# Retention and Fourier-mix kernel on one core: the first batch's constants, DFT tables, scores, folds and mean are rearranged

## The chip, the core and the metric

One core of one Trainium2 chip runs the whole kernel in one launch. Its five engines have queues of their own and are synchronised by semaphores: TensorE (PE, matrix multiply; PEld is its weight load), VectorE (DVE), ScalarE (ACT), GpSimd (POOL) and SyncE (SP), which issues most of the transfers. Sixteen DMA engines move data between HBM and the on-chip memory SBUF; matrix products land in PSUM, in banks[...]. The metric is the device time of one execution in microseconds, as a median over executions. A profile is one more execution, recorded by the hardware.

## The reference

Inputs are q, k, v of shape (4 batches, 8 heads, 768 steps, 64) and two weights, 512 x 2048 and 2048 x 512. The first half is a retention recurrence with one decay per head; the second is a Fourier token mix and a two-layer MLP:

```python
gamma = 1.0 - 2.0 ** (-5.0 - np.arange(H))
for t in range(S):
    state = gamma * state + einsum('bhd,bhe->bhde', k[:, :, t], v[:, :, t])
    y[:, :, t] = (1 / sqrt(D)) * einsum('bhd,bhde->bhe', q[:, :, t], state)
x = y.transpose(0, 2, 1, 3).reshape(B, S, H * D)         # (4, 768, 512)
u = x + np.real(fft(fft(x, axis=1), axis=2))
un = (u - mean(u)) / sqrt(var(u) + 1e-6)                 # over the 512 channels
out = u + np.maximum(un @ w_ch1, 0) @ w_ch2
```

## The kernel before

All four batches run one after another, each in two parts that overlap with the neighbours' parts.

**Attention.** Heads are taken in pairs, so that 2 x 64 channels fill 128 partitions, in the order 0, 3, 1, 2 (`PAIR_ORDER`, L30). The sequence is cut into 6 chunks of 128 steps. For each pair `load_unit` (L91) loads q, k and v, 384 KB each, on SyncE's queue. `cast_unit` (L233) turns them into 16-bit q16, kd (k times a decay per step, from `gexp`) and v16; this runs on GpSimd, but for q of batches 1 to 3, which ScalarE casts (L250) into `q16z`, a layout in which each head has a 128-wide block with zeros in the other head's half. `t_unit` (L261) transposes q and kd: in batch 0 on TensorE through PSUM with a ScalarE copy back, in batches 1 to 3 by DMA on SyncE's queue (L267, L269). `a_unit` (L284) forms the scores of two chunks: because qTz holds zeros in the other head's rows, one 128-row matmul with 256 columns gives both heads, and VectorE multiplies by `maskp`, the causal mask times a decay per head, into `atm`. `kv_unit` (L300) forms the chunk states s16 by a chain of VectorE updates. `y_unit` (L326) adds the part from earlier chunks (qT times s16) and the part within the chunk (atm times v16), and ScalarE scales the sum into x (L349). The 512 channels of x lie on two "sides": 0 holds channels 0 to 256 upward, 1 holds 512 to 256 downward, so that channel c and 512 - c stand at the same place.

**Fourier part.** `fold_unit` (L355) uses the symmetries of a real transform: sums and differences of the two halves of the sequence (`xab`, L367), then of the two sides (`eo`, L371), in two column blocks (columns 0 to 129, and 130 to 257). Stage 1, `s1_unit` (L376), multiplies eo by cosine and sine tables over the sequence (`csp`, `ssp`) into g, and VectorE reverses g into g16r. `g0_unit` (L394) does channel 0 with another layout of the cosines, `csn`. Stage 2, `s2_unit` (L418), multiplies g by the channel tables (`cd16`, `sd16`) for one block of 128 rows, forms u in two VectorE operations, adds x on VectorE or GpSimd (L448, L450), takes mean and variance (`bn_stats`, `bn_aggr`, L453, L454) and lets ScalarE write `un` = mean - u (L456). In batch 0 the first three blocks are transposed on TensorE (`unT_unit`, L472), all others by DMA on SyncE's queue.

**MLP.** `h0_unit` (L505; the first three blocks of batch 0) and `h_unit` (L490) form the first layer in PSUM, relu alternates between ScalarE and VectorE. `ch_unit` (L525) accumulates the second layer over 16 matmuls of 512 columns, scales by 1/sigma from `rstd_unit` (L463) and stores.

**What sets the order.** The program is written as units. At the start come the loads of batch 0 and the constants, then all `trig` units (the five DFT table units: three VectorE operations, an absolute value and two sines on ScalarE each, in four temporary buffers used in turn; and a GpSimd copy that makes csn from csp), then `attn_units(0)`, pair after pair, the weight loads, and the first three stage-2 blocks. From then on `emit` (L596) merges the units of the MLP of batch b, of the attention of batch b + 1 and of their stage 2 by a fraction of the MLP's course. The tile framework takes this order as a priority and makes the order of each engine's queue from it with a plan of its own in which every instruction starts once its inputs are ready; so a unit can stand ahead of one that was written before it. `issue_after` (L242, L544, L553) ties an instruction to a place behind another on its engine: the first casts of batch 1 behind the third block of stage 2, the weight loads (on GpSimd's queue) behind the last casts of batch 0. The loads of batch 1 wait for weight loads, by a dependency that is set by hand (L98 to L102).

The lines that build the zero fills and the constants on the engines before (GpSimd memsets and iotas, ScalarE's maskp) are L113 to L166 and L211 to L227.

## Time and profile before

| | us |
|---|---|
| median of 3 executions | 285.1 (284.24 to 285.47) |
| the profiled execution's time | 284.21 |
| its span, first to last instruction | 282.4 |
| TensorE busy | 235.9 (84%) |
| VectorE busy | 179.1 (63%) |
| ScalarE busy | 111.7 (40%) |
| GpSimd busy | 74.0 (26%) |

The page cuts the span into 40 slices of 7.06 us; a digit is the busy share of a slice in tenths. The lines in order of time read: start in us, duration in us, engine, line of the kernel, operation, what is written <- what is read, shapes, number of instructions merged into the line, and in brackets how long the engine had been idle and what ended that. Ends of TensorE's matmuls are modelled. SPq is SyncE's queue of transfers: a line there is the time in which the transfer was issued, not that in which the data moved.

### The profile page before, as it was taken

The page shows a single profiled execution, that of the slowest core. Times are in us where ns is not written, and L with a number is a line of the kernel's source. Part 1 is how long each engine was busy: PE and PEld are TensorE (multiplying, and loading weights), DVE is VectorE, ACT ScalarE, POOL GpSimd, SP SyncE. Part 2 cuts the span into 40 slices and gives each one's busy share as a digit, 9 for nine tenths or more (in the row PEclk, how much of TensorE's full clock was granted, in tenths as well). Part 3 has the DMA queues.
Part 4 walks back from the last instruction along what each step waited for, and adds up shares of the span by engine and source line. Part 5 has one row for each costly group of instructions (what it writes and reads, how often), then busy time and mean ns, then how long its engine had stood idle before and what let it go on. Part 6 is the DMA issues. An engine that isn't in the chain of part 4 may idle for free.

```text
span 282.4 us, 4877 instructions
## 1 busy us (share of the span) xinstructions
PE 235.9 (84%) x1840; PEld 147.6 (52%) x1840; DVE 179.1 (63%) x424; ACT 111.7 (40%) x228; POOL 74.0 (26%) x145
## 2 busy tenths in 40 slices
PE   1138565749998899979997999989999999899994
PEld 0027453739665565456555654556566546445541
DVE  7666586356296886878768884498788735623421
ACT  4956734264433443545421661244224513511300
POOL 5678300166031122534213041131000501300000
PEclk9999957595999999999999999999999999999999
DMA  9999999999759999599999982134610031112001
GB/s 169 218 218 160 204 192 214 220 218 185 150 121 226 230 222 166 116 231 175 214 244 205 193 161 75 75 67 102 95 74 2 19 111 39 37 56 78 0 37 75
DMA packets 122039, 39.50 MB, mean 140 GB/s; under 512 B 114848, under 2 KB 118944, under 8 KB 122016
## 3 DMA queue, kind: packets, MB, share of 16 engines
q1 hardware_dynamic: 117792, 35.01, 63.5%
q0 software_dynamic: 4224, 4.19, 9.3%
q8 instruction: 14, 0.23, 0.4%
q14 instruction: 9, 0.07, 0.1%
HBM read 27.26 MB, written 6.29 MB: 119 GB/s over the span
## 4 chain that ended last, share of the span: by engine, by line
PE 54%; DVE 17%; ACT 12%; DMA 6%; issue 5%; POOL 3%; SPq 1%; POOLq 0%; ACTq 0%; DVEq 0%
PE psc L532 24%; PE psh L495 14%; PE psh L512 3%; PE wkA L292 3%; DMA qTz<-q16z 3%; PE ps L383 3%; DVE bst L453 2%; DMA q<-in_q_dram 2%; POOL u L450 2%; DVE eo L371 2%; DVE xab L367 2%; DVE atm L294 2%; ACT x L349 2%; PE wkY L337 2%; DVE ht L501 1%
## 5 line engine op out<-in xcount | busy, mean ns | idle before, releaser
L532 PE MATMUL psc<-w,ht 128*128 128x512 f16 x384 | 88.8, 379 | 0.7 <-DVE ht L501 0.7
L495 PE MATMUL psh<-unT,w 128*128 128x384 f16 x448 | 82.7, 326 | 2.3 <-DMA unT<-un 1.5
L532 PEld LDWEIGHTS <-ht 128*128 128x128 f16 x384 | 36.1, 98 | 38.9 <-issue 1.9
L495 PEld LDWEIGHTS <-w 128*128 128x128 f16 x448 | 41.9, 98 | 27.6 <-issue 5.3
L499 ACT ACTIVATE ht<-psh 128x384 f16<-128x384 f32 x56 | 27.3, 489 | 56.9 <-PE psh L495 56.7
L294 DVE TENSOR_TENSOR atm<-wkA,maskp 128x512 f16<-128x512 f32 x48 | 32.7, 684 | 13.3 <-PE wkA L292 13.2
L501 DVE TENSOR_SCALAR ht<-psh 128x384 f16<-128x384 f32 x56 | 30.6, 548 | 9.9 <-PE psh L495 9.9
L536 DVE SCALAR_TENSOR_TENSOR ob<-psc,stats,u 128x512 f32<-128x512 f32 x24 | 17.9, 744 | 29.4 <-PE psc L532 29.4
L448 POOL TENSOR_TENSOR u<-u,x 128x256 f32<-128x256 f32 x21 | 13.4, 637 | 86.6 <-DVE u L442 84.2
L292 PE MATMUL wkA<-qTz,kT 128*128 128x256 f16 x96 | 19.7, 298 | 12.5 <-ACT kT L281 10.9
L252 POOL TENSOR_SCALAR kd<-k,gexp 128x384 f16<-128x384 f32 x32 | 18.7, 595 | 32.9 <-PE wkK L310 8.0
L456 ACT ACTIVATE un<-u,stats 128x512 f16<-128x512 f32 x24 | 17.2, 720 | 22.8 <-DVE stats L454 18.9
L349 ACT ACTIVATE x<-wkY,gexp 128x384 f16<-128x384 f32 x32 | 16.9, 582 | 20.1 <-PE wkY L341 20.0
L450 POOL TENSOR_TENSOR u<-u,x 128x256 f32<-128x256 f32 x24 | 15.6, 650 | 30.4 <-DVE u L444 26.8
L453 DVE BATCH_NORM_STATS2 bst<-u 128x6 f32<-128x512 f32 x24 | 16.6, 694 | 9.4 <-POOL u L450 9.2
L320 DVE SCALAR_TENSOR_TENSOR s<-s,gk,wkK 128x128 f16<-128x128 f16 x64 | 21.7, 339 | 0.5
L337 PE MATMUL wkY<-s,qTz 128*128 128x64 f16 x160 | 17.5, 199 | 4.1 <-DVE s L320 2.9
L337 PEld LDWEIGHTS <-qTz 128*128 128x128 f16 x160 | 13.8, 103 | 11.8 <-issue 4.4
L292 PEld LDWEIGHTS <-kT 128*128 128x128 f16 x96 | 9.5, 105 | 18.5 <-ACT kT L281 11.5
L255 POOL TENSOR_SCALAR v<-v 128x768 f16<-128x768 f32 x16 | 13.6, 847 | 19.4 <-DMA v<-in_v_dram 19.4
L442 DVE SCALAR_TENSOR_TENSOR u<-pq,g,qn 128x257 f32<-128x257 f32 x24 | 11.5, 477 | 10.6 <-ACT qn L439 10.6
L512 PE MATMUL psh<-unT,w 128*128 128x128 f16 x192 | 15.3, 258 | 3.4 <-ACT unT L484 2.5
(101 smaller groups left out, 253.4 us busy)
## 6 DMA issues: line engine op xcount, KB each, us to landing
q<-in_q_dram SPq DMA_DIRECT2D x16, 384.0 KB, 6.1
k<-in_k_dram SPq DMA_DIRECT2D x16, 384.0 KB, 6.2
v<-in_v_dram SPq DMA_DIRECT2D x16, 384.0 KB, 6.2
out_dram<-ob SPq DMA_DIRECT2D x24, 256.0 KB, 2.2
w<-in_moe_w_ch_dram POOLq DMA_DIRECT2D x8, 512.0 KB, 10.9
unT<-un SPq DMA_TRANSPOSE x21, 2.4
qTz<-q16z SPq DMA_TRANSPOSE x12, 4.1
kT<-kd SPq DMA_TRANSPOSE x12, 2.9
```

Source lines behind the costliest of these rows:

```text
L292: nc.tensor.matmul(wk[:, c2], st["kT"][:, c, :], st["qT"][:, c], start=True, stop=True)
L294: nc.vector.tensor_tensor(out=st["atm"][:, 2 * part:2 * part + 2], in0=wk, in1=maskp[:, PAIR_ORDER[i]].unsqueeze(1).to_broadcast([P, 2, 2, ...
L320: nc.vector.scalar_tensor_tensor(out=s16[:, c], in0=s16[:, c - 1], scalar=gk128[:, hp:hp + 1], in1=wk[:, c - c0], op0=ALU.mult, op1=ALU.add)
L337: nc.tensor.matmul(yk[h2][:, c, :], qT[:, c, h2, :], s16[:, c - 1, sl], start=(c == 1), stop=False, skip_group_check=True)
L349: nc.scalar.activation(dst, yk[h2], AF.Copy, bias=0.0, scale=gq8[:, h:h + 1])
L450: xadd = nc.gpsimd.tensor_tensor(out=u[:, kb, 256:512], in0=u[:, kb, 256:512], in1=x[:, kb, 1, 257:1:-1], op=ALU.add)
L453: nc.vector.bn_stats(bst, u[:, kb, :])
L495: nc.tensor.matmul(psh, w116[:, cb, fb * P:(fb + 1) * P], unT[:, cb, rt * 384:(rt + 1) * 384], start=(cb == 0), stop=(cb == 3))
L499: nc.scalar.activation(ht16[:, fb, :], psh, AF.Relu, bias=0.0, scale=-1.0)
L501: nc.vector.tensor_scalar(out=ht16[:, fb, :], in0=psh, scalar1=-1.0, scalar2=0.0, op0=ALU.mult, op1=ALU.max)
L512: nc.tensor.matmul(psh[:, f], w116[:, cb, fb * P:(fb + 1) * P], unT[:, cb, kb * P:(kb + 1) * P], start=(cb == 0), stop=(cb == 3))
L532: nc.tensor.matmul(psc, ht16[:, fb, rb3 * P:(rb3 + 1) * P], w216[:, fb, :], start=(fb == 0), stop=(fb == NFB - 1))
```

## The change

The edits concern batch 0 and the constants.

- **Constants over the engines.** Fewer index patterns on GpSimd (one instruction for several columns); the memsets of `lgrow`, `gk128` and `maskf` go to VectorE; the decay table `gexp` comes ahead of the identity, of the long index row `kf` and of the other constants. The eight ScalarE copies that make `maskp` and the zero fills of `q16z` move into `late_consts`, written after the third stage-2 block; the zero fills of `qTz` are dropped (the DMA transposes of q16z write the zeros). Six small VectorE operations for row parity move into `parity_consts`, behind pair 1.
- **DFT tables between the pairs.** Ten temporary buffers in place of four; two table units after each of the pairs 0 and 1, one after pair 2. csn is made by three more sines on ScalarE in place of the GpSimd copy.
- **Row-tiled scores.** In batch 0 q is transposed without zeros by one ScalarE copy for both heads; each head's scores are a 64-row matmul of 128 columns (head 0 in partitions 0 to 63, head 1 in 64 to 127) into a PSUM bank of its own, three chunks at a time, and VectorE multiplies by a constant and the plain mask `maskf`. The state part of y is done on 64 rows too.
- **Folds by side.** The fold is split into `fold_s` (sums and differences of the sequence halves, for given columns and sides) and `fold_d`. In batch 0 everything that does not need the last pair is folded before the last pair's y. Batches 1 to 3 do the same operations as before.
- **Mean from sums of x.** For the first three blocks the mean of u is computed as (sum of x) / 512 plus the channel-0 spectrum g0. ScalarE sums x while copying it to a scratch tile; `bn_stats` and `bn_aggr` for the three blocks move into `rstd_unit`, ahead of the square root.

```diff
-    ident16 = const.tile([P, P], f16, tag="ident16")
-    make_identity(nc, ident16)
...
-    for c in range(3):
-        nc.gpsimd.iota(icol_i[:, c:c + 1], pattern=[[0, 1]], base=P * c, channel_multiplier=1)
-    for c in range(2):
-        nc.gpsimd.iota(icol_i[:, 3 + c:4 + c], pattern=[[0, 1]], base=P * c + 1,
-                       channel_multiplier=1)
...
+    tmp2 = up.tile([P, NCH, DM], f32, tag="u32", name="tmp2")
...
+    rs = [tmp[:, 2 + n] if n < 4 else tmp2[:, n - 4] for n in range(10)]
...
+    nc.gpsimd.iota(icol_i[:, 0:3], pattern=[[P, 3]], base=0, channel_multiplier=1)
+    nc.gpsimd.iota(icol_i[:, 3:5], pattern=[[P, 2]], base=1, channel_multiplier=1)
+    nc.gpsimd.iota(icol_i[:, 5:6], pattern=[[0, 1]], base=127, channel_multiplier=-1)
     for h in range(H):
-        nc.gpsimd.memset(lgrow[:, h:h + 1], float(lng[h]))
-    gexp = const.tile([P, 2, H], f32, tag="gexp")
+        nc.vector.memset(lgrow[:, h:h + 1], float(lng[h]))
+    nc.vector.memset(maskf, 1.0)
+    nc.vector.tensor_copy(icol[:, 0:6], icol_i[:, 0:6])
     nc.vector.tensor_scalar(out=gexp[:, 0], in0=lgrow, scalar1=icol[:, 3:4],
                             scalar2=float(math.log(0.125)), op0=ALU.mult, op1=ALU.add)
...
     nc.scalar.activation(gexp, gexp, AF.Exp, bias=0.0, scale=1.0)
...
+    make_identity(nc, ident16)
...
+    nc.gpsimd.iota(kf_i, pattern=[[1, KN]], base=0, channel_multiplier=0)
+    nc.vector.tensor_copy(kf, kf_i)
...
+    for hp in range(NHP):
+        nc.vector.memset(gk128[0:64, hp:hp + 1], float(gam[2 * hp] ** P))
+        nc.vector.memset(gk128[64:128, hp:hp + 1], float(gam[2 * hp + 1] ** P))
...
+    def late_consts():
+        for h in range(H):
+            nc.scalar.activation(maskp[:, h // 2, h % 2], maskf, AF.Copy, bias=0.0,
+                                 scale=float(gam[h] ** (-P)))
+        for j in range(2):
+            nc.vector.memset(qzs[j][:, :, 0, D:P], 0.0)
+            nc.vector.memset(qzs[j][:, :, 1, 0:D], 0.0)
...
+    def parity_consts():
...
     def trig_unit(idx, n, w, col, coln, emit):
-        r = tmp[:, 2 + idx % 2, 0:w]
-        ra = tmp[:, 4 + idx % 2, 0:w]
+        r = rs[2 * idx][:, 0:w]
+        ra = rs[2 * idx + 1][:, 0:w]
...
+            nc.scalar.activation(csn[:, c, :], ra[:, 0:384], AF.Sin, bias=hpi, scale=-sc)
...
-    def trig_end():
-        nc.gpsimd.tensor_copy(csn.rearrange("p c (i t) -> p c i t", t=2),
-                              csp[:, :, :, 0:192].rearrange("p t c i -> p c i t"))
-    trig.append(trig_end)
...
-        nc.vector.memset(qz[:, :, 0, D:P], 0.0)
-        nc.vector.memset(qz[:, :, 1, 0:D], 0.0)
...
-        nc.vector.memset(qt[D:P, :, 0, :], 0.0)
-        nc.vector.memset(qt[0:D, :, 1, :], 0.0)
...
     def t_unit(b, i):
...
-                if nm == "qT":
-                    for h2 in range(2):
-                        sl = slice(D * h2, D * h2 + D)
-                        nc.scalar.copy(qT[sl, :, h2, :], tq[sl])
-                else:
-                    nc.scalar.copy(kT, tq)
+                nc.scalar.copy(dst, tq)
         return run
+
+    def a0_unit(i, half):
+        def run():
+            st = at[0, i]
+            hp = PAIR_ORDER[i]
+            if half == 0:
+                st["atm"] = ap_.tile([P, NCH, 2, P], f16, tag="atm", name="atm")
+            wk = [ps_g.tile([P, 3, P], f32, tag="g", name="wkA", padded_shape=[P, 4, P])
+                  for _ in range(2)]
+            for c3 in range(3):
+                c = 3 * half + c3
+                for h2 in range(2):
+                    sl = slice(D * h2, D * h2 + D)
+                    nc.tensor.matmul(wk[h2][:, c3, :], st["kT"][sl, c, :], st["qT"][sl, c, :],
+                                     start=True, stop=True)
+            for h2 in range(2):
+                nc.vector.scalar_tensor_tensor(
+                    out=st["atm"][:, 3 * half:3 * half + 3, h2, :], in0=wk[h2],
+                    scalar=float(gam[2 * hp + h2] ** (-P)),
+                    in1=maskf.unsqueeze(1).to_broadcast([P, 3, P]),
+                    op0=ALU.mult, op1=ALU.mult)
+        return run
...
     def y_unit(b, i):
...
+                    if b == 0:
+                        lhsT, rhs = qT[sl, c, :], s16[sl, c - 1, sl]
+                    else:
+                        lhsT, rhs = qT[:, c, h2, :], s16[:, c - 1, sl]
+                    nc.tensor.matmul(yk[h2][:, c, :], lhsT, rhs,
...
-    def fold_unit(b, cb):
+    def fold_s(b, lo, hi, s0, s1):
...
+            for a, op in ((0, ALU.add), (1, ALU.subtract)):
+                nc.vector.tensor_tensor(out=ab[:, a, :, s0:s1, lo:hi],
+                                        in0=x[:, 0:3, s0:s1, lo:hi],
+                                        in1=x[:, 3:6, s0:s1, lo:hi], op=op)
+        return run
+
+    def fold_d(b, cb):
...
+    def xmean_unit(kb):
+        def run():
+            if kb == 0:
+                fd[0]["xm"] = stt.tile([P, 4], f32, tag="xm", name="xm")
+            junk = up.tile([P, 2, 257], f16, tag="un16", name="junk")
+            nc.scalar.activation(junk, xts[0][:, kb, :, 1:258], AF.Copy, bias=0.0, scale=1.0,
+                                 accum_out=fd[0]["xm"][:, kb:kb + 1])
+        return run
+
+    def mean_unit():
+        xm = fd[0]["xm"]
+        mu = fd[0]["mu"] = stt.tile([P, 4], f32, tag="mu", name="mu")
+        nc.vector.scalar_tensor_tensor(out=mu[:, 0:3], in0=xm[:, 0:3], scalar=1.0 / DM,
+                                       in1=fd[0]["g0"][:, 0:3], op0=ALU.mult, op1=ALU.add)
...
+            if b == 0 and kb < 3:
+                una = nc.scalar.activation(un, u[:, kb, :], AF.Identity,
+                                           bias=fd[0]["mu"][:, kb:kb + 1], scale=-1.0)
+                lb[b]["bst", kb] = bst
+            else:
...
     def rstd_unit(b, rt):
...
+            if b == 0 and rt == 0:
+                for kb in range(3):
+                    bst = lb[0].pop(("bst", kb))
+                    nc.vector.bn_stats(bst, lb[0]["u"][:, kb, :])
+                    nc.vector.bn_aggr(stats[:, kb, 0:2], bst)
...
+    def first_units():
+        un = []
+        for i in range(4):
+            un += [cast_unit(0, i), t_unit(0, i), a0_unit(i, 0), kv_unit(0, i), a0_unit(i, 1)]
+            if i == 3:
+                un += [fold_s(0, 0, 130, 0, 2), fold_s(0, 130, 258, 0, 1), fold_d(0, 0),
+                       g0_unit(0), s1_unit(0, 0, 0), s1_unit(0, 1, 0)]
+            un.append(y_unit(0, i))
+            if i < 3:
+                un += trig[2 * i:2 * i + 2]
+            if i == 1:
+                un.append(parity_consts)
+        un += [xmean_unit(0), fold_s(0, 130, 258, 1, 2), fold_d(0, 1), s1_unit(0, 0, 1),
+               s1_unit(0, 1, 1), xmean_unit(1), xmean_unit(2), mean_unit]
         return un
...
-    for u in trig:
-        u()
-    for u in attn_units(0):
+    for u in first_units():
         u()
...
     for u in (s2_unit(0, 0), s2_unit(0, 1), unT_unit(0, 0), s2_unit(0, 2)):
         u()
+    late_consts()
```

## The prediction

> **What bounds the kernel now.** I read the page first, then the program in order of time from 0 to 92 us, then the SyncE queue alone, then the chain of waits. The page says that this is a TensorE kernel with a slow start:
>
> ```profile
> span 282.4 us, 4877 instructions
> ...
> PE   1138565749998899979997999989999999899994
> ...
> ACT  4956734264433443545421661244224513511300
> ...
> DMA  9999999999759999599999982134610031112001
> ```
>
> A slice is 7.06 us. TensorE is full only from slice 9 (64 us); the DMA engines are full from 0 to about 70 us. The change edits only what runs before that. Two clocks therefore matter: when the first batch's arithmetic lets the first MLP matmul start, and when the DMA engines deliver the second batch. The order of time shows the first clock and what delays it:
>
> ```profile
> 17.64 0.49 ACT L195 ACTIVATE cd<-tmp,hpi 128x257 f16<-128x257 f32 x1
> 18.16 0.80 ACT L281 COPY kT<-tq 128x768 f16<-128x768 f16 x1
> 19.01 0.61 PE L292 MATMUL wkA<-qTz,kT 128*128 128x256 f16 x2 [7.88 <-ACT kT L281]
> ...
> 24.45 0.83 POOL L255 TENSOR_SCALAR v<-v 128x768 f16<-128x768 f32 x1 [0.23 <-DMA v<-in_v_dram]
> ...
> 40.54 1.05 ACT L349 ACTIVATE x<-wkY,gexp 128x384 f16<-128x384 f32 x2 [4.07 <-PE wkY L341]
> ...
> 52.37 4.47 PE L512 MATMUL psh<-unT,w 128*128 128x128 f16 x48
> ```
>
> The first head pair's scores start at 19.0, when ScalarE has finished every DFT table, though its transposes were over at 11.1. The last pair's v has landed at 24.45 but its outputs reach x only at 41.6: work lags data by 16 us. The first MLP matmul runs at 52.37. The second clock:
>
> ```profile
> 55.35 0.93 ACT L250 CAST q16z<-q 128x384 f16<-128x384 f32 x2 [4.30 <-DMA q<-in_q_dram]
> ...
> 57.71 1.05 PE L512 MATMUL psh<-unT,w 128*128 128x128 f16 x16 [0.87 <-ACT ht L517]
> ...
> 64.10 9.82 PE L512 MATMUL psh<-unT,w 128*128 128x128 f16 x128 [2.54 <-ACT unT L484]
> ```
> ```profile
> 63.29 1.69 SPq L96 DMA_DIRECT2D v<-in_v_dram  x1
> 65.15 3.25 SPq L267 DMA_TRANSPOSE qTz<-q16z  x1
> ```
>
> A cast of the second batch sits in ScalarE's queue ahead of the un of block 1 and waits for its load; TensorE stalls behind it. The second batch's transposes are behind all its loads on SyncE, so they start at 65.15 and TensorE takes that batch's first scores at 78.08.
>
> **What the skill says.** "TensorE: Matmul & The Clock Gate", Part 1 (queue depths): ScalarE and VectorE are strict FIFO. The trace agrees: the cast at 55.35 held two later ScalarE instructions that needed none of its data. "ScalarE: Activation LUTs", What ACT_TABLE_LOAD costs: a load takes 1283 ns, an ACTIVATE with immediates 186 + 0.833 N ns, with a pointer operand 280 + 0.833 N. The trace agrees: 1.28 us; at N = 386 the Sin of ssp takes 0.536 (0.508 by the page) and that of csp, with a pointer bias, 0.627 (0.602). "TensorEngine Tiling (Array Packing)", Key Properties: row tiles run concurrently, and a change of tiling mode drains the array. No instruction of the kernel before is row-tiled, so that is unmeasured here.
>
> **The change part by part.**
>
> *Constants.* Eight VectorE zero fills (0.92 to 3.75, 2.8 us) leave the front of VectorE; GpSimd's six small iotas become three, and its 8 lgrow and 8 gk128 memsets and the maskf fill go to VectorE. The Exp at 5.69 needed icol (3.75), then 0.82 + 0.12 us of gexp. Now icol can be copied at about 2.5 after some 9 memsets; Exp at about 4, 1.7 us earlier. kd of pair 0 ran at 9.10 behind v; k must have landed near 6.5 (v landed at 8.29, loads are 1.8 us apart), so kd gains about 2.6 us. The moved memsets cost VectorE under 2 us where it waits for data anyway; uncovered they would be that. Identity moves later on GpSimd but is needed only at 5.57.
>
> *DFT tables.* ScalarE's table work keeps its 15 activations (7.7 us: 1.6 + 1.6 + 1.9 + 0.8 + 0.8 + 1.0, and the 1.28 load) and gains three 384-wide Sin for csn, priced by the csp row at 0.63 each (1.6 in sequence); GpSimd loses the 1.20 us copy. They now have lower priority than the pairs. Between 4 and 25 ScalarE has 21 us: tables 10.6, the new copies 4 x 1.6, three pairs' s and x 3 x 1.35: 21.1 in all, less some 0.1 us that each of about 35 starts before the one in front has ended, so it just fits. Cost on the path: nothing if so, up to 2 us if the last table is left over. VectorE's 8.7 us of table arithmetic loses its wait for old buffers (2.46 us) and fills the idle time before pair 0.
>
> *Transposed q.* Two 64-partition copies of 0.79 us per pair become one of 0.80: 3.2 us of ScalarE saved, 0.8 of it in the last pair's path.
>
> *Scores.* Per pair 3 VectorE products of 0.687 (512 wide) become 4 of 384: 0.687 - 128/0.96 ns = 0.55, so 2.2 against 2.06. TensorE: 6 matmuls of 256 columns become 12 of 128 on half the rows. At the slow cadence (0.85 us for 4, or 0.21 each) this is 1.28 now; bounds are 0.65 if halves overlap perfectly and 2.4 if every load is exposed and modes drain. I take 1.3; GpSimd's input rate of 5.4 us per pair covers the rest. The state matmuls of y are row-tiled likewise.
>
> *Folds.* After the last y, two 768-wide xab (0.55 each) become two 384-wide (0.55 - 192/960 us = 0.35): 0.4 us saved. The other half is done in front of y, on VectorE, where 3.3 us of folds compete with the last pair's products.
>
> *Mean.* bn_stats and bn_aggr (0.69 + 0.17) leave the path to the first three un; three ScalarE sums of 514 elements come in, 186 + 0.833 x 514 = 0.61 us estimated from the page's price, with an unknown accumulator read. They stand in ScalarE's gaps (4.35 busy of 11.2 us in 41 to 52.2); if the last two delay the first qn they cost 1.3 and undo the gain. The statistics return before the square root; first needed at 77.4.
>
> *Late constants.* 8 maskp copies (1.8 us) and 4 fills leave the front; ScalarE's idle time before the un covers them, else 1.5.
>
> *The sum.* Loads are unchanged: last k near 22.7, last v 24.45. kd 1.15, transposes 0.8, kT 0.8, scores 0.6 give first products at 26.1. VectorE then needs 4 x 0.55 + 5 x 0.30 = 3.7 plus up to 1.3 of folds: 31.1. y 0.8, x 1.06: 33.0. Remaining fold and first eo 1.2, other eo 0.5, s1 2.0, g 0.6: 36.8. pq 0.4, qn 0.4, u 0.9, x added 0.7: 39.2. un 0.72, transpose 0.5, copy 0.4: about 41. That is 11.4 us before 52.37. w1 is in time: its last quarter has landed by 36.7, when SyncE's next load, which waits for it, is issued.
>
> Not all reaches the end. q of pair 1 of batch 2 still lands at 55.3 and SyncE's loads still end at 65.0. The first layer takes 192 x 0.077 (9.82 us for 128) and the first three second-layer blocks 48 x 0.217: 25 us, so TensorE has work until 66, or 70 if that cast holds it for some 4 us as it does now; then it waits for nothing but the second batch's transposes: 65.15 + 4.1 us gives scores at about 70, against 78.08. The 28.5 us from there to that batch's last y (106.6), the 6 to its s2 and the rest of the chain are unchanged and move as a block; TensorE has about 59 us of work in that stretch (14.7 first half of the first layer, 10.4 = 64 x 0.163 second, 20.8 = 96 x 0.217 second layer, 13 for the second batch's attention and spectra), and 74 us between 41 and the 115 that replaces 123, so it keeps up. Gain 78.1 - 70 = 8.1 us. Afterwards each batch repeats with a 55.5 us period (second-layer runs start at 112.6, 168.1, 223.6), so the shift stays. The profiled execution is 284.21 us (282.4 span, 1.8 around it): 276.1 there; its time is 0.9 under the median 285.1, so 277.0.
>
> **The rivals.**
>
> *Late transposes or another head-of-line wait keeps part (0.20).* The cast for batch 2 may again stand ahead of an un, so that the MLP restarts at 56 to 57. It then runs densely to about 68 instead of 73.7, since 60.7 to 64.1 need not be lost again: gain 3 to 5.5, 279.5 to 282. For it: the data cannot come earlier. Against: the first un now run 10 us before the data.
>
> *No effect (0.07).* The second batch's chain after 86 us contains waits for DMA (qTz 3.5 us, a load 6.7 us). If those set its end independently of its start, the 8 us are given back: 284 to 286.
>
> *Slower (0.12).* The planner may place the second batch's scores early in TensorE's queue. They cannot run before 69.5. At 69.5 the kernel before has 134 of these 192 first-layer matmuls behind it (64, and 5.4 us of the run from 64.1); if the scores stood ahead of all of them, 134 x 0.077 = 10.3 us of work would be left that now is done: 295. It decides where fewer than 134 stand ahead. For: the code's own order puts them after about 9 first-layer units. Against: in the kernel before all 192 and 20 more ran first.
>
> *More (0.06).* If TensorE's lead shortens the second batch's chain as well, up to 12 to 14: 271 to 273.
>
> **How the numbers follow.** The forecast case has 0.55: 277.0, its own range 273 to 280, from the unknowns (2 us tables, 1.3 sums, 1.5 masks, up to 1.1 for the tiled scores of the last pair; 3 us of chain shortening above). Adding the partial case to 282 and the flat one gives 271 to 285 for 8 in 10. Half a per cent, 1.4 us, is about what a measurement of this kernel can tell from no change. Faster 0.81, same 0.07, slower 0.12.
>
> **What would show it.** Right: kT of pair 0 copied near 9; last x near 33; first psh near 41; the loads of batch 2 still to about 65; its first wkA near 70; second-layer runs 55.5 us apart and all about 8 us earlier. Wrong: ScalarE's tables still running when the last kT is wanted; the tiled matmuls taking over 2.4 us a pair; a long TensorE idle before 70 with first-layer matmuls queued behind scores; or a first psh near 41 with second-layer runs not moved.

## The result, and the profile after

The changed kernel is slower: 288.14 us (median of 4 runs, 287.53 to 288.73) against 284.67 us for the kernel before, measured beside it on the same chip. The ratio is 1.0126, with a 95% interval of 1.008 to 1.0171. The forecast was 277.0 us with a range of 271 to 285, so both the sign and the range were wrong. The profiled execution took 288.02 us, with a span of 286.3. Three single executions below were over 1.5% longer than the fastest of their kernel and are left out of the ratios, though not of the medians: 285.9 us for the joined kernel, 286.96 for the changed one with the wider stretch and 295.21 for the joined one with its stores on GpSimd.

The page of the changed kernel, in slices of 7.16 us:

```profile
span 286.3 us, 4925 instructions
...
PE   1497757699759989899949969989999999999994
...
ACT  4798264530354424555131552244214513511400
...
PEclk9999999979958999999997999999999999999999
DMA  9999999999799997889988983225410031112001
```

TensorE is full from slice 8 (57 us) now, earlier than before. But slices 10 and 11 (72 to 86 us), full before, show 7 and 5, and in slice 11 the granted clock falls to half; slice 20 (143 to 150 us) shows 4. The order of time, with the instructions that answer to those shown of before:

```profile
11.35 0.80 ACT L275 COPY kT<-tq 128x768 f16<-128x768 f16 x1 [1.78 <-PE tq L273]
...
35.75 1.05 ACT L369 ACTIVATE x<-wkY,gexp 128x384 f16<-128x384 f32 x2
...
46.01 4.46 PE L563 MATMUL psh<-unT,w 128*128 128x128 f16 x64
...
63.32 10.52 PE L583 MATMUL psc<-w,ht 128*128 128x512 f16 x48
73.68 0.38 PE L308 MATMUL wkA<-qTz,kT 128*128 128x256 f16 x2
```

The first kT is copied at 11.35 instead of 18.16, the last x is written from 35.75 instead of 40.54, and the first MLP matmul starts at 46.01 instead of 52.37, 6.4 us earlier. The second layer of block 0 starts 10.4 us earlier (73.76 before). Then all 48 of its matmuls run before the second batch's first scores; in the kernel before 20 did. SyncE's queue:

```profile
65.38 4.03 SPq L265 DMA_TRANSPOSE qTz<-q16z  x1
69.46 1.27 SPq L267 DMA_TRANSPOSE kT<-kd  x1
```

The second batch's first transposes start when they did before (65.15).

The second-layer runs that the prediction names, with the second batch's first layer between them, in the changed kernel:

```profile
109.65 7.93 PE L583 MATMUL psc<-w,ht 128*128 128x512 f16 x36
...
120.36 5.46 PE L546 MATMUL psh<-unT,w 128*128 128x384 f16 x32 [1.40 <-DMA unT<-un]
...
171.52 10.52 PE L583 MATMUL psc<-w,ht 128*128 128x512 f16 x48
...
227.39 10.52 PE L583 MATMUL psc<-w,ht 128*128 128x512 f16 x48
```

And in the kernel before, from the second batch's first scores on:

```profile
78.08 0.38 PE L292 MATMUL wkA<-qTz,kT 128*128 128x256 f16 x2
...
112.48 7.93 PE L532 MATMUL psc<-w,ht 128*128 128x512 f16 x36
...
123.06 5.36 PE L495 MATMUL psh<-unT,w 128*128 128x384 f16 x32 [1.49 <-DMA unT<-un]
...
168.04 10.52 PE L532 MATMUL psc<-w,ht 128*128 128x512 f16 x48
...
223.52 10.52 PE L532 MATMUL psc<-w,ht 128*128 128x512 f16 x48
```

The lead of 6.4 us is 4.4 at the second batch's first scores, 2.7 at its first layer and -3.5 at its last second-layer run (171.52 against 168.04). Most of it is lost between 120 and 171 us, around slice 20.

The stretches with the two thin places by their windows: busy time and count of TensorE, its weight loads, VectorE, ScalarE, GpSimd, then the granted clock, the DMA share and GB/s. First the changed kernel, then the kernel before:

```profile
core 0: us, PE busy (x) PEld busy (x) DVE busy (x) ACT busy (x) POOL busy (x), PEclk, DMA share, GB/s
74.00:86.00 12.00, 7.29 (x67) 4.97 (x65) 10.66 (x28) 5.55 (x11) 3.56 (x6) 0.68 0.90 181
...
143.00:172.00 29.00, 22.46 (x163) 13.52 (x162) 18.18 (x43) 10.84 (x24) 6.90 (x11) 0.94 0.91 166
```
```profile
74.00:86.00 12.00, 12.00 (x94) 6.77 (x93) 8.91 (x21) 3.52 (x9) 2.42 (x4) 1.00 0.62 121
...
143.00:172.00 29.00, 27.01 (x212) 16.12 (x211) 21.94 (x53) 11.93 (x26) 8.48 (x13) 1.00 0.92 187
```

From 74 to 86 us TensorE stands idle for 4.7 us and runs at a clock of 0.68, while VectorE is busy for 10.66 of the 12 us with that batch's attention. The kernel before filled this stretch with second-layer matmuls; the changed one has used them up. That is not yet a loss: work done earlier is not due later, and the lead falls by only 1.7 us over the whole way from the scores to the first layer. From 143 to 172 us TensorE is idle for 6.5 us instead of 2.0, and there it falls behind.

### The profile page after: what moved, and what is told of

It reads as the page before. It is cut to its first block, busy times and chain, and to the rows that moved or that the text cites. A ratio compares the mean times of both kernels' runs of the same rounds, so it can differ in the third digit from the quotient of the medians.

```text
span 286.3 us, 4925 instructions
## 1 busy us (share of the span) xinstructions
PE 242.7 (85%) x1864; PEld 149.0 (52%) x1864; DVE 176.3 (62%) x444; ACT 111.3 (39%) x233; POOL 71.5 (25%) x124
## 4 chain that ended last, share of the span: by engine, by line
PE 44%; DVE 11%; DMA 6%; ACT 4%; POOL 3%; issue 2%; SPq 0%; POOLq 0%; ACTq 0%
PE psc L583 22%; PE psh L546 15%; DMA qTz<-q16z 4%; DVE bst L500 2%; DVE xab L386 2%; PE wkA L308 2%; DMA q<-in_q_dram 2%; POOL u L490 2%; PE ps L423 2%; DVE ht L552 1%; POOL u L488 1%; ACT x L369 1%; DVE u L482 1%; PE wkY L357 1%; ACT ht L550 1%
## 5 line engine op out<-in xcount | busy, mean ns | idle before, releaser
L546 PE MATMUL psh<-unT,w 128*128 128x384 f16 x448 | 83.8, 328 | 5.1 <-ACT ht L550 2.6
L583 PEld LDWEIGHTS <-ht 128*128 128x128 f16 x384 | 37.1, 99 | 42.2 <-issue 3.5
L550 ACT ACTIVATE ht<-psh 128x384 f16<-128x384 f32 x56 | 27.2, 488 | 63.2 <-PE psh L546 61.9
L310 DVE TENSOR_TENSOR atm<-wkA,maskp 128x512 f16<-128x512 f32 x36 | 24.4, 682 | 14.1 <-PE wkA L308 14.1
L250 POOL TENSOR_SCALAR kd<-k,gexp 128x384 f16<-128x384 f32 x32 | 18.6, 590 | 44.3 <-DMA k<-in_k_dram 27.1
L502 ACT ACTIVATE un<-u,stats 128x512 f16<-128x512 f32 x21 | 15.1, 721 | 18.1 <-DVE stats L501 14.9
L357 PE MATMUL wkY<-s,qTz 128*128 128x64 f16 (+1 forms) x160 | 16.6, 204 | 6.3 <-DVE s L336 4.0
L500 DVE BATCH_NORM_STATS2 bst<-u 128x6 f32<-128x512 f32 x21 | 14.6, 694 | 11.5 <-POOL u L490 11.5
L248 ACT CAST q16z<-q 128x384 f16<-128x384 f32 x24 | 11.3, 512 | 26.0 <-issue 12.0
L357 PEld LDWEIGHTS <-qTz 128*128 128x128 f16 (+1 forms) x160 | 12.2, 103 | 13.2 <-issue 7.7
L308 PE MATMUL wkA<-qTz,kT 128*128 128x256 f16 x72 | 14.7, 294 | 2.2 <-DMA qTz<-q16z 1.5
L386 DVE TENSOR_TENSOR xab<-x 128x780 f16<-128x780 f16 (+2 forms) x18 | 9.6, 582 | 9.8 <-ACT x L369 9.8
```

Source lines behind the costliest of these rows:

```text
L250: nc.gpsimd.tensor_scalar(out=kd[:, :, h2, :], in0=k32[:, h2], scalar1=gkd[:, h0 + h2:h0 + h2 + 1], scalar2=1.0, op0=ALU.mult, op1=ALU.mult)
L308: nc.tensor.matmul(wk[:, c2], st["kT"][:, c, :], st["qT"][:, c], start=True, stop=True)
L310: nc.vector.tensor_tensor(out=st["atm"][:, 2 * part:2 * part + 2], in0=wk, in1=maskp[:, PAIR_ORDER[i]].unsqueeze(1).to_broadcast([P, 2, 2, ...
L357: nc.tensor.matmul(yk[h2][:, c, :], lhsT, rhs, start=(c == 1), stop=False, skip_group_check=True)
L500: nc.vector.bn_stats(bst, u[:, kb, :])
L546: nc.tensor.matmul(psh, w116[:, cb, fb * P:(fb + 1) * P], unT[:, cb, rt * 384:(rt + 1) * 384], start=(cb == 0), stop=(cb == 3))
```

## The experiments

Each kernel was timed beside the kernel before on the same chip, and the ratios are to that. Starts are read from the traces. "Joined" means that the two fold units of batches 1 to 3 are one unit again, as in the kernel before.

**The folds of the later batches.** They do the same operations as before, but the split made them two units instead of one. A batch's list has 37 units instead of 35, and as units are merged with the first-layer and second-layer units at equal fractions of a stretch, each unit's place shifts. First, the changed kernel with its folds joined:

```
-put(fold_s(b, 0, 130, 0, 2), fold_d(b, 0), g0_unit(b), ...
+put(both(fold_s(b, 0, 130, 0, 2), fold_d(b, 0)), g0_unit(b), ...
-put(fold_s(b, 130, 258, 0, 2), fold_d(b, 1), s1_unit(b, 0, 1), ...
+put(both(fold_s(b, 130, 258, 0, 2), fold_d(b, 1)), s1_unit(b, 0, 1), ...
```

> The changed kernel, with the two fold units of batches 1 to 3 run as one unit, as before the change; batch 0 keeps every edit. Theory A (the split lengthens the attention list of later batches from 35 to 37 units, shifts where each of them is merged into the MLP, and the later loss comes from that): first MLP matmul at 46 as in the changed kernel, lead of 2.7 us where batch 1's first layer starts (about 120.4) and still there at the last second-layer run, so about 282 us. Theory B (any other course of the first batch gives another plan of the later ones, and the split is innocent): the lead is lost again after 120, 286 to 289 us.

Measured: 280.7 us, ratio 0.9899 (0.9873 to 0.9925). Joining gives back 7.4 us (6.4 by the ratios, each to the kernel before on its own chip). This version beats both kernels. Second, the kernel before with its `fold_unit` of batches 1 to 3 put as two units:

> The kernel before, with the folds of batches 1 to 3 in two units, batch 0 untouched. Theory A: first MLP matmul at 52.4 as before, and the loss of 4 to 6.6 us appears between 123 and 172: 288 to 291 us. Theory B: within 1.5 us of 284.7, since the first batch runs as before.

Measured: 285.16 us, ratio 1.0057 (1.0037 to 1.0076). The same split costs the kernel before only 1.6 us (by the ratio): it isn't a price that adds to the rest.

Third, the split kept, but the stretch of merging widened by 37/35, so that unit n stands about where it stood before. The stage-2 units of the next batch, whose stretch starts at the end of this one, move with it:

```
-a0, a1 = (0.12, 0.7) if b == 0 else (0.04, 0.62)
+a0, a1 = (0.12, 0.733) if b == 0 else (0.04, 0.653)
```

> The changed kernel with its folds of batches 1 to 3 still in two units each; only the stretch over which the attention units are merged is widened, from 0.62 to 0.653 of a batch (0.7 to 0.733 ahead of batch 1), so that unit n of 37 stands where unit n of 35 stood before. No instruction is added or left out. Theory P (what the split costs is the shift of places in the queues): most of the 7.4 us between the changed kernel (288.1) and the one with joined folds (280.7) comes back, 280 to 284, and the first-layer run of block 1 of batch 1 starts near 148 instead of 154. Theory S (two units of their own cost, wherever they stand): 286 to 289. In between, or beyond both, it is neither: the time then depends on the order in a way that no single place explains.

Measured: 283.48 us, ratio 0.9991 (0.996 to 1.0023). So 4.7 of the 7.4 us (3.8 of 6.4 by the ratios) were the places and not the units. Block 1's first layer in batch 1 starts at 149.0 instead of 154.2, as theory P said.

**The loads.** Three of the four loads of w2 are left out, in the changed kernel and in the kernel before. A fill by GpSimd stands in their place, and the loads of batch 1 that waited for them wait for an earlier weight load (`(3, 5, 7, 7)` becomes `(3, 4, 4, 4)`):

```
+if g:
+    nc.gpsimd.memset(w216[:, 4 * g:4 * g + 4, :], 0.01)
+    return
 w_dma.append(nc.gpsimd.dma_start(w216[:, 4 * g:4 * g + 4, :], ...
```

> The changed kernel, leaving out three of the four loads of the second weight (GpSimd fills that part of the tile with a constant), which takes 3.1 MB of reads off the DMA engines while the second batch is loaded. Theory C (the second batch's loads cap what the first batch's lead can bring): the last load of batch 1 is issued about 12 us earlier than 63.5, batch 1's first scores near 64 and not 73.5, and batch 1's first layer starts 6 to 10 us before 120.4. Theory D (the order of the queues, not the data, sets it): first scores still above 70 and the first layer of batch 1 within 3 us of 120.4.

> The kernel before with the same three loads of the second weight left out. Theory C: its first MLP matmul stays near 52.4 and batch 1's first scores near 72 to 78, since there the first batch and not the data is late; so it gains at most 3 us and stands 5 us or more behind the changed kernel without these loads where batch 1's first layer starts. Theory D: the two stand within 3 us of each other there.

Measured: 286.49 us (ratio 1.0112, 1.0082 to 1.0141) and 277.43 us (0.9792, 0.9756 to 0.9828). Two lines of the changed kernel without these loads, SyncE's first and TensorE's:

```profile
57.52 3.45 SPq L265 DMA_TRANSPOSE qTz<-q16z  x1
```
```profile
63.49 10.09 PE L583 MATMUL psc<-w,ht 128*128 128x512 f16 x46 [0.26 <-DVE ht L570]
73.42 0.38 PE L308 MATMUL wkA<-qTz,kT 128*128 128x256 f16 x2
```

The transposes come 7.9 us earlier and the scores don't move, since 46 second-layer matmuls stand ahead of them. So the arrival of the data isn't the only limit at 73 us; TensorE's order is one too. The joined kernel with the same loads left out came later:

> The changed kernel with joined folds, leaving out three of the four loads of the second layer's weights (a fill by GpSimd in their place), to be held against the kernel before with the same left out (277.4; first MLP matmul at 52.0, first layer of batch 1 at 116.9). If the 39.5 MB that the DMA engines move, and not the order, eat the lead of the first batch, then without these 1.5 MB the lead shows: first MLP matmul near 48.5 as in the split one, time 271 to 274. If it is the order in the queues: 276 to 281.

Measured: 279.75 us (0.9854, 0.9806 to 0.9903), 2.3 us more than the kernel before with these loads left out (1.8 by the ratios). Without this data the lead is lost all the same.

**The second batch's scores earlier.** In the joined kernel the loads of batch 1 are merged over a longer stretch (`l1` 0.1 to 0.25), which puts the first transposes ahead of six loads. In a second kernel only the attention's stretch starts earlier (`a0` 0.12 to 0.08), with the loads left as they are.

> The changed kernel with joined folds (280.7), and the loads of batch 1 merged over -0.1 to 0.25 of batch 0 instead of -0.1 to 0.1. SyncE then issues the first transposes of batch 1 ahead of that batch's last six loads, and TensorE has that batch's first scores ahead of the last 33 first-layer matmuls and of all 48 second-layer matmuls of block 0, instead of behind them. Theory Q (the order in the queues sets when the second batch's attention starts, and its length of some 45 us is its own): first scores at 62 to 66 instead of 73.2, first layer of batch 1 7 to 11 us earlier than 118.3, time 270 to 275. Rival W (TensorE's work sets the time: what is passed must be done later, 33 x 0.077 + 48 x 0.22 = 13 us): first scores early, but the first layer of batch 1 at 116 to 120, time 278 to 284.

> The changed kernel with joined folds (280.7), and the attention of batch 1 merged from 0.08 of batch 0 instead of 0.12. The first scores of batch 1 then stand ahead of 64 first-layer matmuls and all 48 second-layer ones, while the transposes stay behind all loads. This is the slower rival of the forecast made real: TensorE must wait for data at 71 to 72 us with 64 x 0.077 + 48 x 0.22 = 15 us of work behind it. Theory W (TensorE's work sets the time): idle from about 57 to 71, time 290 to 296. Theory Q (the chain of the second batch sets it): first scores at 71.5 to 72.5, time 278 to 282.

Measured: 280.87 us (0.9852, 0.9799 to 0.9905) and 294.65 us (1.0329, 1.0241 to 1.0418). First scores of the first one and its window ahead of batch 1's first layer, then first scores of the second one:

```profile
61.97 0.39 PE L308 MATMUL wkA<-qTz,kT 128*128 128x256 f16 x2 [1.64 <-DMA kT<-kd]
```
```profile
102.00:118.30 16.30, 10.85 (x66) 6.08 (x66) 12.51 (x32) 5.99 (x13) 8.01 (x13) 0.85 0.80 165
```
```profile
71.39 0.61 PE L308 MATMUL wkA<-qTz,kT 128*128 128x256 f16 x2 [13.39 <-DMA kT<-kd]
```

With early scores TensorE is busy for 11.50 us of the stretch from 74 to 86, so the thin place there is gone, but the 11.2 us gained at the scores are gone by the first layer of batch 1 (118.8, against 118.3 without): it now stands idle for 5.5 us just ahead of that. So theory Q falls; start and time are those of rival W. The second kernel is the prediction's slower rival made real: TensorE waits 13.39 us in one place, and 11 us of it reach the first layer of block 1 (95.4 instead of 84.1).

Next, the end of that attention's stretch is moved forward as well (`a1` 0.7 to 0.6 ahead of batch 1):

> The kernel with early scores of the run before (280.9: joined folds, first scores of batch 1 at 62.0, last y of batch 1 at 98.7, first layer of batch 1 at 118.8), with the end of that attention's stretch moved from 0.7 to 0.6 of batch 0. In every kernel so far the second-layer matmuls of block 1 of batch 0 begin within 3 us of the last y of batch 1: the merge puts that y behind all first-layer matmuls of block 1. Theory M (the place in the merge holds the last y back, whatever the first scores do): last y at 93 to 96, first layer of batch 1 at 113 to 116, time 276 to 279. Rival T (the 16 to 20 us from the last y to the first layer are what stretches: its waits on ScalarE's and SyncE's queues): last y earlier, but first layer of batch 1 still at 117 to 120, time 279 to 283.

Measured: 281.34 us (0.9897, 0.9842 to 0.9953). The last y comes at 99.7, no earlier than without the edit (98.7), and the first layer of batch 1 at 118.3. Theory M falls; the time fits rival T, though not its earlier y.

**The parts of the first batch**, each undone alone in the joined kernel: the tables made ahead of the pairs again (`un = list(trig) + [parity_consts]`), the mean from the statistics again, and the scores over 128 rows with two copies of q (and with the mask table, the zero fills and the state part of y that go with them). A fourth kernel puts `y_unit(0, 3)` ahead of `g0_unit` and `s1_unit`.

> The changed kernel with joined folds (280.7), and the DFT tables with the parity constants made ahead of the first head pair again, with three table activations more than the kernel before had. If the place of the tables is what brings the first MLP matmul forward: kT of pair 0 copied at 19 to 20 instead of 11.4, first MLP matmul 3 to 5 us later than 46.2, time 283 to 286. If the last pair's loads (v landed at 24.5) set the end of the first batch's attention: kT of pair 0 late, but the first MLP matmul within 1 us of 46.2, time 280 to 282.

> The changed kernel with joined folds (280.7; first MLP matmul at 46.2), with the mean of the first three blocks from the statistics again: the three sums and the mean's instruction are left out, the two statistics instructions stand ahead of each un again. If the mean from sums shortens the path to the first MLP matmul as the forecast had it, by 0.69 + 0.17 us: first MLP matmul at 47, time 281 to 282. If the sums on ScalarE (0.82 us each with the read of the accumulator) cost as much as they save: first MLP matmul at 45.5 to 46.4, time unchanged.

> The changed kernel with joined folds (280.7; first MLP matmul at 46.2), with the scores of batch 0 as in the kernel before: q transposed into the half-empty layout by two copies of a pair, products over all 128 rows, the mask table and the zero fills made at the start. If the row tiling and the single copy are what the first batch gained by: kT of pair 0 some 0.8 us later, last x 2 to 4 us later than 37.1, first MLP matmul at 48 to 50, time 282 to 285. If it is worth little: first MLP matmul within 1 us of 46.2, time 280 to 282.

> The changed kernel with joined folds (280.7), with the channel-0 product and the first spectra of batch 0 placed behind the last y instead of ahead of it in the order of the code. In the changed kernel the last y's products wait some 2.2 us behind these matmuls on TensorE. If that is what part of the forecast's first step lost: last x about 2 us earlier than 37.1, first MLP matmul 1 to 2 us earlier than 46.2, time 279 to 280.7. If what is passed is then late itself: first MLP matmul at 46 to 47.5, time 280.5 to 282.

| joined kernel, with | first MLP matmul | time, us | ratio (95%) |
|---|---|---|---|
| nothing else | 46.2 | 280.7 | 0.9899 (0.9873 to 0.9925) |
| tables ahead | 47.3 | 281.49 | 0.9868 (0.9791 to 0.9945) |
| mean from statistics | 48.1 | 285.19 | 1.0055 (1.0027 to 1.0083) |
| scores over 128 rows | 49.3 | 281.12 | 0.9898 (0.9848 to 0.9949) |
| last y ahead | 44.3 | 286.33 | 1.0076 (1.0051 to 1.01) |

The last kernel's x and first MLP matmul:

```profile
34.20 1.05 ACT L369 ACTIVATE x<-wkY,gexp 128x384 f16<-128x384 f32 x2 [4.64 <-PE wkY L361]
```
```profile
44.31 3.87 PE L563 MATMUL psh<-unT,w 128*128 128x128 f16 x45
```

Each part moves the first MLP matmul in the expected direction: the tables are worth 1.1 us there, the mean 1.9, the scores with their copies 3.1, and the wait of the last y 1.9. But the time doesn't follow. The earliest start has the longest time, and a start 3.1 us later costs nothing that can be measured. Three of the four expectations missed the time; for the tables a start 3 to 5 us later was expected, and it was 1.1. Over these five kernels the end doesn't follow the start of the MLP.

**A chain through SyncE?** In the changed kernel, this stands around the channel-0 product of batch 2 (TensorE, then SyncE, then ScalarE):

```profile
149.02 0.36 PE L445 MATMUL ps<-xg,csn 128*128 128x4 f16 x9 [3.92 <-DVE xg L440]
...
150.56 1.91 PE L583 MATMUL psc<-w,ht 128*128 128x512 f16 x4
...
167.97 0.81 PE L546 MATMUL psh<-unT,w 128*128 128x384 f16 x4 [1.36 <-ACT ht L550]
```
```profile
161.72 0.57 SPq L93 DMA_DIRECT2D q<-in_q_dram  x1
```
```profile
166.48 0.51 ACT L248 CAST q16z<-q 128x384 f16<-128x384 f32 x1 [3.34 <-DMA q<-in_q_dram]
```

And in the kernel before, with the last second-layer run ahead of it:

```profile
145.37 3.62 PE L532 MATMUL psc<-w,ht 128*128 128x512 f16 x16
...
150.57 0.36 PE L405 MATMUL ps<-xg,csn 128*128 128x4 f16 x9 [1.58 <-DVE xg L400]
```

The same run of 16 ends 3.9 us earlier in the changed kernel (it starts at 141.47). But the x that the product needs are written by 145.80 instead of 147.48, only 1.7 us earlier. TensorE therefore waits 3.92 us with eight ready second-layer matmuls behind the product, and four of those then take 1.91 us, where four take 1.03 at full clock. A store of their output waits on SyncE until 154.86, with transposes and the last loads of batch 3 behind it; a cast of that q waits for 3.34 us on ScalarE, and TensorE for what is behind the cast. To test the store's link, the stores were issued by GpSimd (`nc.gpsimd.dma_start(out[...], ob)`), in the changed kernel and in the joined one:

> The changed kernel (288.1, folds in two units), with the stores of the output issued by GpSimd instead of SyncE. In the changed kernel a store that waits for the last second-layer matmuls stands in SyncE's queue until 154.86, and the transposes of the third pair of batch 2 and the last loads of batch 3 stand behind it; the second-layer run of block 1 of batch 1 begins at 171.5. Theory H (the late g0 product delays that store, the store the loads, the load a cast and the second layer): with the stores out of SyncE's queue the last loads of batch 3 are issued near 157 instead of 161.7, the run begins at 167 to 169, time 283.5 to 286. Rival N (the store is not in that chain; VectorE's and TensorE's queues alone set it): run at 170.5 to 172, time 287 to 289.

> The changed kernel with joined folds (280.7), with the stores issued by GpSimd. Under theory H the store costs less here (it stood until 149.2), 278.5 to 280.5; under rival N 280 to 282. Slower than 282 would say that the stores on GpSimd hold up its casts.

Measured: 292.06 us (1.0276, 1.0218 to 1.0334) and 292.08 us (1.0257, 1.0199 to 1.0315). Batch 3's last v is issued at 153.87 instead of 163.76 in the first of them, and still the second-layer run of block 1 starts at 172.5 (171.5 in the changed kernel):

```profile
153.87 2.18 SPq L93 DMA_DIRECT2D v<-in_v_dram  x1
```

So the late loads alone don't explain that start, and theory H isn't supported. Neither is rival N: 292 lies above both, and batch 1's first layer started 3.3 us later, so moving the stores changed more than the link under test.

**The order alone.** A control without any edit of an instruction, the kernel before with the wider stretch; then its counterpart with the first batch's edits, the joined kernel with the wider stretch; then the wider stretch with the early scores:

> A control: the kernel before with no edit of its instructions, only the stretch of merging widened from 0.62 to 0.653 of a batch (0.7 to 0.733 ahead of batch 1), as in the changed kernel with the wider stretch. If the order of merging alone moves the time by as much as the first batch's edits were to bring: 2 us or more away from the kernel before, to either side. If the kernel before is robust to it and only the changed one is not: within 1.5 us of it.

> The changed kernel with joined folds and the wider stretch of merging (0.653, and 0.733 ahead of batch 1): the counterpart, with the first batch's edits, of the control on the kernel before (280.8). Together they give the worth of those edits in a third order of merging; in the order of the kernel before it is some 3 us (284.2 to 280.7), in the order with split folds it is a loss of some 3 us (285.2 to 288.1). If the edits are worth their 3 us in any order that suits them: 277 to 279. If about 280.7 is what these queues allow, whatever the start: 280 to 282. If the sign depends on the order: above 282.

> The same wider stretch in the kernel with the early scores of batch 1 (280.9). If a fuller TensorE around 60 to 80 us and the wider stretch add up: 277 to 279.5. If about 280.7 is what these queues allow: 280 to 282. Above 282 if the order turns against it.

Measured: 280.81 us (0.9887, 0.9856 to 0.9918), 285.83 us (1.0083, 1.0048 to 1.0117) and 280.76 us (0.9909, 0.9884 to 0.9933). The kernel before gains 1.1% by the order alone, about as much as the joined kernel with all the edits (1.0%). Four pairs now differ in the first batch's edits at one order each:

| order of the later batches | without the edits | with them | lead at first MLP matmul | at first scores of batch 1 | at its first layer | at its last second-layer run | at the last such run of all |
|---|---|---|---|---|---|---|---|
| of before | 1 | 0.9899 | 6.2 | 4.9 | 4.8 | 3.3 | 3.3 |
| split folds | 1.0057 | 1.0126 | 6.4 | 4.5 | 3.2 | -2.7 | -2.7 |
| wider stretch | 0.9887 | 1.0083 | 7.0 | 3.7 | 1.4 | -4.1 | -5.2 |
| fewer loads | 0.9792 | 0.9854 | 4.4 | -0.6 | -0.1 | -1.6 | -1.6 |

(The last five columns are starts without the edits minus starts with them, in us.) The edits win 1.0% in one order and lose 0.7 and 2.0% in two others, each beyond the intervals. The loss of 0.6% with fewer loads is not clear of them (0.9756 to 0.9828 and 0.9806 to 0.9903). In each pair the lead is there at the first MLP matmul, shrinks by 1.3 to 5.0 us up to the second batch's first scores, and by another 1.5 to 5.9 us between the first layer and the last second-layer run of that batch; after this it moves by 1.1 us at most. Window 74 to 86 us of the joined kernel, of the one with the wider stretch, and of the control:

```profile
74.00:86.00 12.00, 6.99 (x72) 4.84 (x70) 10.25 (x28) 6.21 (x13) 3.56 (x6) 0.89 0.92 185
```
```profile
74.00:86.00 12.00, 5.77 (x62) 4.00 (x60) 10.30 (x29) 5.56 (x11) 3.53 (x6) 0.77 0.95 188
```
```profile
74.00:86.00 12.00, 11.31 (x92) 6.45 (x91) 8.83 (x21) 3.05 (x7) 2.42 (x4) 1.00 0.72 145
```

With the edits TensorE is short of 5 to 6 us of work here; without them it is nearly full. The joined kernel wins with this gap and the one with the wider stretch loses with it, so the gap by itself doesn't decide.

**Idle time and clock.** From the first MLP matmul to the end, the changed kernel, the joined one and the kernel before:

```profile
46.01:286.30 240.29, 215.74 (x1611) 129.81 (x1609) 145.17 (x338) 81.71 (x170) 50.38 (x79) 0.96 0.64 128
```
```profile
46.18:279.10 232.92, 212.63 (x1611) 127.88 (x1609) 143.72 (x338) 81.85 (x170) 51.72 (x79) 0.98 0.65 132
```
```profile
52.37:282.40 230.03, 211.78 (x1612) 128.74 (x1610) 144.34 (x334) 82.49 (x171) 50.13 (x79) 0.97 0.62 127
```

In these single executions the changed kernel needs 10.3 us more than the kernel before for nearly the same matmuls: TensorE is idle for 24.6 us instead of 18.3, and busy for 4.0 us longer. Against the joined kernel, which has the same matmuls, it is idle for 4.3 us more and busy for 3.1 us longer, at a granted clock of 0.96 and not 0.98. So not all of the loss is waiting; some of it goes with slower running.

**What stays open.** That the order of the later batches decides the worth of the lead is shown by the pairs. Which single place in which queue takes it between 118 and 171 us isn't. In the changed kernel the trace names three: 2.3 us of longer wait at the channel-0 product of batch 2, the halved clock behind it, and 2.55 us of waits for the relu (1.36, 0.31 and 0.88) ahead of the second-layer run at 171.52, where the kernel before has none. Over the kernels the first of them doesn't go with the time: the wait at the channel-0 product of batch 2 is 3.92 us in the changed kernel and 3.21 in the edited one with the wider stretch, and only 2.12 in the joined one and 0.89 in the control, but 1.58 in the kernel before, which is slower than both. With the stores on GpSimd the changed kernel had only 0.06 us of it and was still slower, but there more was moved. No run changed that wait alone. Seven kernels lie between 280.7 and 281.5 us with starts from 45.8 to 52.2; that they share a bound was not shown.

## Why the prediction was wrong

The step that failed is the last of the sum: "Afterwards each batch repeats with a 55.5 us period (second-layer runs start at 112.6, 168.1, 223.6), so the shift stays." It took the later batches for a fixed train that moves with its start. In the changed kernel these runs start at 109.65, 171.52 and 227.39: the first is 2.8 us earlier than before, the second follows after 61.9 us and is 3.5 us later, and only the third keeps the period (55.9). The pairs of the last table show why no period could be relied on: with the same first-batch edits, the order of the later batches alone turns a lead of 6 to 7 us into a gain or a loss.

Of the 8.1 us of the forecast, 3.7 were missing at the second batch's first scores already. The part that was to "move as a block" behind them nearly did: from the first scores to the first layer of that batch it took 46.7 us instead of 45.0. Then 6.2 us went up to the run at 171.52.

- *First MLP matmul at 41*: it came at 46.0. The Exp at about 4 (3.39), the products of 0.55 us, the halved folds (0.36), the sums of 0.61 (0.63) and the loads' end at 65 were right. The kd of pair 0 gained nothing: GpSimd casts v first still (8.17) and kd at 9.10, as before, so kT came at 11.35 and not near 9. The last x ended at 36.8 and not at 33.0. About 1.9 us of that were the last y's products behind the spectra's matmuls in TensorE's queue, a wait that the sum left out and that the run with y ahead took away. The stretch from there took 9.2 us instead of 8.0. The sum itself has a slip: 33.0 and its terms 1.2, 0.5, 2.0 and 0.6 make 37.3 and not 36.8, so with its later terms (2.4 and 1.6) the first MLP matmul would stand at 41.3.
- *First scores of batch 1 at 70*: they came at 73.7. The sum allowed for the transposition of q (4.03 us) and forgot that of k behind it (1.27 us). Where TensorE waited for nothing else it started on this data at 71.4. The rest is TensorE's order: 48 second-layer matmuls stood ahead, where the forecast assumed that TensorE would be waiting.
- *TensorE keeps up, with 59 us of work in 74*: from 46.0 to 120.4 it was busy for 63.7 us of 74.4, so the amount was nearly right. What was wrong is that capacity settles it: with enough work in sum TensorE still stood idle for 4.7 us from 74 to 86, where its second-layer work was already done, and for 6.5 us from 143 to 172.
- *Late constants.* They were not late: the planner placed four of the eight mask copies at 2.10 to 4.20 on ScalarE, the others at 24.16, and the four fills at 2.09 to 2.93 on VectorE, ahead of icol (2.85). The place in the code did not take them off the front.
- *"Batches 1 to 3 do the same operations as before"* in the description was true, and from it the forecast took that nothing changes there. Two units more in a list shift the place of each later unit. Joining them moved the time by 7.4 us (6.4 by the ratios), not much less than the whole forecast gain of 8.1.
- *The rivals.* The slower rival had the right sign by a mechanism that the changed kernel doesn't show; built, it took 294.65 us where 295 was worked out. The rival of no effect named the cause best, waits of the second batch that don't depend on its start, and was given 0.07.
- *The range* took in what could be added up ahead of 86 us. It had no term for the order of the later batches, though the control shows that this alone moves the kernel before by 3.4 us.

## What to carry to other kernels

An edit that saves time at the front of a kernel with in-order queues can be worth nothing, or less, at the end: here a lead of 6 to 7 us became 3.3 us or turned into a loss. Ask whether the next batch's data and the work behind it move too, what TensorE will do with the time gained, and what it will lack later. Where units are merged by fractions of a list, count the units: a list longer by two is an edit of every batch. Before trusting a gain or loss of 1 to 2%, measure what a change of order alone does to the kernel before, and judge the edit in more than one order.

## What the runs showed of the hardware

Row tiles beside transposes of the full array, and the sums, from the changed kernel:

```profile
10.49 0.82 PE L273 MATMUL tq<-ident,kd 128*128 128x128 f16 x6 [4.05 <-POOL kd L250]
...
12.20 0.50 PE L290 MATMUL wkA<-qTz,kT 64*128 64x128 f16 x6 [0.89 <-ACT kT L275]
```
```profile
36.83 0.63 ACT L406 ACTIVATE junk<-x 128x514 f16<-128x514 f16 x1
37.37 0.19 ACT L406 ACTIVATION_READ_ACCUMULATOR junk<-x 128x1 f32 x1
```

- Six products of 64 rows and 128 columns took 0.50 us, where six transposes of 128 columns over the full array took 0.82 just before. A pair's twelve took about 1.0 us; the forecast took 1.3 between bounds of 0.65 and 2.4. The Trainium skill's "TensorEngine Tiling (Array Packing)", Key Properties, says that different tiles can run in parallel; the trace agrees, with the 0.50 beside the 0.82. What the change of mode costs is not measured here.
- Each sum on ScalarE is followed by a read of the accumulator, an instruction of its own of 0.18 to 0.19 us, behind 0.61 to 0.63 for 514 elements.
- On VectorE in the kernel before, 512 columns took 0.744 us (L536) and 257 took 0.477 (L442), or 1.05 ns a column. The forecast's 0.55 us for 384 columns fits this; it measured 0.551.

Three windows of the changed kernel, in which the granted clock is the last number but two:

```profile
75.00:78.00 3.00, 1.43 (x15) 0.86 (x14) 3.00 (x9) 0.84 (x3) 1.92 (x4) 1.00 0.45 90
79.00:84.00 5.00, 2.24 (x13) 1.13 (x11) 4.77 (x15) 2.98 (x6) 0.82 (x2) 0.50 1.26 247
...
150.20:153.40 3.20, 3.20 (x12) 1.54 (x11) 1.54 (x4) 0.35 (x1) 0.00 (x0) 0.51 1.18 234
```

- The third begins 1.2 us after the wait of 3.92 us that ends at 149.02. TensorE was busy throughout at 0.51 of its clock, and four second-layer matmuls took 1.91 us instead of 1.03; some 1.6 us were lost, an estimate from the 3.20 us and the 0.51. "TensorE: Matmul & The Clock Gate", Part 1, has TensorE at half its clock after an idle window of some 3.4 us; this place agrees.
- The second does not quite: the clock was 0.50 there too, though in the first window, just ahead of it, TensorE was busy for 1.43 of 3 us and no single wait was longer than 0.46. A row of short gaps was followed by the lower clock as well, so gaps can cost more than their own length.
